# A first MLP block begun pair of heads by pair of heads, with two PSUM banks for the early scores and a new order of instructions

## The chip, the cores and the metric

The kernel runs on one core of a Trainium2 chip. The metric is the device time of one execution in microseconds (us). Its engines are named as the profile names them: PE (TensorE) with its weight loads (PEld), DVE (VectorE), ACT (ScalarE), POOL (GpSimd) and SP (SyncE), whose queue issues most of the DMAs. PE writes its results to PSUM, which has eight banks; the program calls them `bank[0]` to `bank[7]` and the profile calls all of them `pb`.

## What is computed

Four batches of 576 positions go through local attention, a convolutional gated MLP, and a Fourier mix with a second MLP. Cut to what matters:

```python
def attention(q, k, v):                    # (4, 8, 576, 64)
    scores = matmul(q, k.T) / sqrt(64)
    # heads 0-3: the last 32 keys; heads 4-7: 32 keys at distances 0, 4, 8, ...
    scores = where(mask, scores, -1e9)
    a = exp(scores - scores.max(-1))
    return matmul(a / (a.sum(-1) + 1e-9), v)

def first_mlp(x, w_in, conv_w, w_out):     # x (4, 576, 512), w_in (512, 1024)
    h = relu(x @ w_in)
    c = conv3(h, conv_w)                   # along the positions, each of 1024 columns by itself
    return (h * sigmoid(c)) @ w_out

def second(x, w_ch1, w_ch2):               # w_ch1 (512, 2048)
    u = x + real(fft(fft(x, axis=1), axis=2))
    un = (u - mean(u)) / sqrt(var(u) + 1e-6)
    return u + relu(un @ w_ch1) @ w_ch2
```

The weights come as 64-bit floats. Matrix products are made of three products of rounded parts: each operand is split into a high part and a low part (`h`, `l`), and high x high, high x low and low x high are added up.

## The kernel before, in words

**Attention in ticks.** `tick` (L586) handles one piece of a pair of heads: 3 ticks for each of a batch's two plain pairs and 4 for each of its two dilated pairs, 14 a batch, numbered 0 to 55. A tick is a chain: PE adds the mask and the scores into a bank (`sb`); ACT copies them to a tile `sm` (one of a ring of five; from batch 2 on DVE does this and adds the mask); POOL takes the maximum over the partitions into `mx`; DVE subtracts; ACT takes the exponential; PE multiplies with V into a second bank (`pb`); ACT and DVE make the reciprocal `rs`; ACT (L627) or DVE (L624) scales into `xb`; PE transposes; ACT writes the high part of `x` and DVE the low part. A batch's `x` is a tile `xT[b]` of four pairs, `xT[b][:, c]` for pair c. Pair 0 comes from ticks 0 to 2, pair 1 from 3 to 5, pair 2 from 6 to 9, pair 3 from 10 to 13.

**First MLP.** `mlp1` (L1109) goes through eight blocks f of 128 columns. `m1(b, f)` (L666) multiplies `x` with the weight tile (0, f) in two halves of 288 positions. A half is four pairs c times three products, twelve matmuls of 128x288, added up in one bank, which ACT evicts with a relu into `hp`. ACT and DVE then make the convolution `cv`, the gate `g` and the split product `hid`. `m2(b, f)` (L695) multiplies `hid` with the weight tile (1, f) into the accumulators in banks 4 to 7, over all eight f; after the last one they are copied out (`evac`, L742). The sixteen weight tiles are converted from 64 bits, by `Weights.convert` (L534): three DVE steps on `raw` and `win`, a copy to `wf` on ACT or POOL, and a DVE subtraction into the low part of `wf`. Two `raw` tiles take turns.

**Banks.** `of(group, ids)` (L481) hands out banks in turn. The first 16 ticks (`EARLY`, L1092) take their scores in banks 0, 2, 3 and 4 and their second products in 1, 5, 6 and 7; later ticks use bank 0, and 1 and 3. `m1` uses bank 2 in the batches 0 to 2.

**Order.** The program first lists all its work as `Work` entries, with the tiles that each reads and writes, and then a planner (`Plan.order`, L306) lays them out. An entry has engines that could do it, an estimated duration and a key, its due time; `products` (L257) gathers the matmuls made under it into one entry, so that they stand together on PE and wait together. `urgency` (L299) lowers keys so that an entry is due before those that need it. The planner simulates the engines and gives each free one, among the entries that are ready, the one with the lowest key. Then each engine's instructions are issued in that order, and on the chip each waits for what it needs. Between two passes of `urgency` the keys are shaken: each number of `NUDGES` (L188) seeds a random stretch of time and an amplitude, and keys in that stretch are moved by a random amount. The list is what a search over seeds has left.

The times that set the keys here are `at = 1.6 * n` for the ticks of batch 0, `T0 - 8 + 66 / 14 * m` for tick m of batch 1, and

```python
T0 = 42.0
PER = 69.0
        step = PER / NF1
            at = T0 + PER * b + step * f
            m1(b, f, h_banks, at)
            m2(b, f, at + 2 * step)
```

Most of the profile's lines are helpers: L253 is every DVE, ACT and POOL operation recorded by `run`, L266 every PE operation, L295 every DMA. Tiles tell them apart: `pb<-QT,KT` and `pb<-maskt,ident` are scores, `pb<-VT,sm` the second product of a tick, `pb<-ident,xb` its transposes, `pb<-x,wf` is `m1`, `pb<-wf,hid` is `m2` and the last product of the second MLP.

Of the kernel before, what the change touches and what calls it, by code (L numbers as in the profile page):

```python
# [182 lines left out]
class Work:  # L183
# [1 line left out]

NUDGES = (9, 12, 27, 33, 49, 53, 82, 92, 98, 130, 181, 284, 297, 353, 473,  # L188
          503, 521, 594, 836, 1456, 1870, 2106, 2119, 2189, 2250, 2504, 2667, 2792, 3014, 3080,
          3211,)  # L190


LAT = {"PE": 0.25, "DVE": 0.12, "ACT": 0.15, "POOL": 0.2, "SP": 0.0, "NO": 0.0}
# [5 lines left out]
class Plan:  # L199
# [79 lines left out]
    def mm3(self, o, ah, al, bh, bl, first, last):  # L279
        self.mm(o, ah, bh, first, False)  # L280
        self.mm(o, ah, bl, False, False)
        self.mm(o, al, bh, False, last)
# [23 lines left out]
    def order(self):  # L306
        W = self.works
        for w in W:
            w.succ, w.left, w.ready, w.start = [], len(w.deps), 0.0, None
        for w in W:  # L310
            for d in w.deps:
                W[d].succ.append(w.id)
        self.urgency()
        for seed in NUDGES:
            rng = random.Random(seed)
            a = rng.uniform(0, 560)
            z = a + rng.uniform(4, 50)
            amp = rng.choice((1, 2, 4, 8))
            for w in W:
                if a < w.key < z:  # L320
                    w.key += rng.uniform(-amp, amp)
        self.urgency()
        free = dict.fromkeys(("PE", "DVE", "ACT", "POOL", "SP", "NO"), 0.0)
        can = {e: {} for e in free}
        bus, drift = 0.0, 0.0
        out = []

        def can_wait(w, end):
            return w.key < 1e8 and end < w.key + min(w.where.values()) + drift

        def offer(w):
            for e in w.where:
                can[e][w.id] = w
        for w in W:
            if not w.left:
                offer(w)
        while any(can.values()):
            best = None
            for e, c in can.items():
                if c:  # L340
                    t = max(free[e], min(w.ready for w in c.values()))
                    if best is None or t < best[0]:
                        best = t, e
            t, e = best
            pick = None

            wait = WAIT.get(e, 0.0)
            for w in sorted((w for w in can[e].values() if w.ready <= t + wait + 1e-9), key=lambda w: w.key):
                late = False
                for e2, us in w.where.items():  # L350
                    if e2 != e:
                        queue = sum(x.where[e2] for x in can[e2].values()
                                    if x.key < w.key and x.ready <= t and len(x.where) == 1)
                        if max(free[e2], t) + queue + us < t + w.where[e] - 1e-9 and not (
                                us < w.where[e] and can_wait(w, t + w.where[e] + 0.5)):
                            late = True
                if not late:
                    pick = w
                    break
            if pick is None:  # L360

                free[e] = min([f for x, f in free.items() if f > t + 1e-9] + [t + 0.3])
                continue
            w = pick
            for x in w.where:
                del can[x][w.id]
            t = max(t, w.ready)
            w.start, w.eng = t, e
            if e == "PE":
                drift += 0.1 * (t - w.key - drift)  # L370
            end = t + w.where[e]
            free[e] = end
            if w.bytes:
                begin = max(bus, end)
                bus = begin + w.bytes / 265e3
                end = bus + 2.0
            out.append(w)
            for s in w.succ:
                x = W[s]
                lat = 0.0 if w.bytes else LAT[e] if e not in x.where else 0.0  # L380
                x.ready = max(x.ready, end + lat)
                x.left -= 1
                if not x.left:
                    offer(x)
        assert len(out) == len(W), [w.id for w in W if w.start is None][:5]
        return out
# [51 lines left out]
def tile_kernel(ctx: ExitStack, tc: tile.TileContext, forms, qt_in, ktp, ktd, vtp, vtd, wm1, wm2, conv_w,  # L438
# [3 lines left out]
    P = Plan({"ACT": nc.scalar, "DVE": nc.vector, "POOL": nc.gpsimd, "PE": nc.tensor, "SP": nc.sync})  # L442
    mm, mm3, dma = P.mm, P.mm3, P.dma
# [11 lines left out]
    def copy(out_, in_, engines=("ACT",), key=None):  # L455
        n = out_.n()
        psum = in_.tile.pool is banks
        t = {"ACT": on_act(n), "DVE": on_dve(n, False, psum), "POOL": on_pool(n)}
        P.run({e: t[e] for e in engines}, "copy", key, out=out_, in_=in_)

    def dve(op_, us, key=None, **kw):
        P.run({"DVE": us}, op_, key, **kw)

    def lo_of(out_, src, hi, key=None):
        n, psum = out_.n(), src.tile.pool is banks
        dve("tensor_tensor", on_dve(n, True, psum), key, out=out_, in0=src, in1=hi.bitcast(F32), op=ALU.subtract)
# [14 lines left out]
    def of(group, ids):  # L481
        i = turns.get(group, 0)
        turns[group] = i + 1
        return bank[ids[i % len(ids)]]
# [84 lines left out]
    def kq_load(u):  # L569
        b, hp = divmod(u, 4)  # L570
        kt, qt = KT[u % NS], QT[u % NS]
        i = 2 * b + hp % 2
        dma(kt[:, 0:608] if hp < 2 else kt, ktp[i] if hp < 2 else ktd[i])
        dma(qt[0:64, 0, :], qt_in[u, 0:64])
        dma(qt[64:128, 1, :], qt_in[u, 64:128])
# [7 lines left out]
    xT = {b: x_even if b % 2 == 0 else x_odd for b in range(B)}  # L583
# [82 lines left out]
    def m1(b, f, h_banks, at):  # L666
        s = NF1 * b + f
        w = W1.tiles[0, f]
        hp = hpad[s % 2]
        for half in range(2):  # L670
            o = of("h", h_banks)[:, :HS]
            sl = slice(HS * half, HS * half + HS)
            with P.products(at + 4.3 * half):
                for c in range(4):
                    wsl = slice(128 * c, 128 * c + 128)
                    mm3(o, w[:, 0, wsl], w[:, 1, wsl], xT[b][:, c, 0, sl], xT[b][:, c, 1, sl], c == 0, c == 3)
            P.run({"ACT": 0.41}, "activation", out=hp[:, 1 + HS * half:1 + HS * half + HS], in_=o, func=AF.Relu,
                  scale=0.5)
        cv, g = cv_t, g_t
        P.run({"ACT": 0.78}, "mul", out=cv, in_=hp[:, 1:S + 1], mul=convw[:, NF1 + f:NF1 + f + 1])  # L680
        dve("scalar_tensor_tensor", 0.81, out=cv, in0=hp[:, 0:S], scalar=convw[:, f:f + 1], in1=cv,
            op0=ALU.mult, op1=ALU.add)
        dve("scalar_tensor_tensor", 0.88, out=cv, in0=hp[:, 2:S + 2],
            scalar=convw[:, 2 * NF1 + f:2 * NF1 + f + 1], in1=cv, op0=ALU.mult, op1=ALU.add)
        P.run({"ACT": 0.69}, "activation", out=cv, in_=cv, func=AF.Tanh)
        dve("scalar_tensor_tensor", 0.54, out=g[:, 0:289], in0=cv[:, 0:289], scalar=1.0, in1=hp[:, 1:290],
            op0=ALU.add, op1=ALU.mult)
        dve("scalar_tensor_tensor", 0.48, out=g[:, 289:576], in0=cv[:, 575:288:-1], scalar=1.0,
            in1=hp[:, 576:289:-1], op0=ALU.add, op1=ALU.mult)
        gh, gl = hid[s] = gh_t[s % 2], gl_t[s % 2]  # L690
        gs = g.rearrange("p (t s) -> p t s", t=2)
        copy(gh, gs, ("ACT", "POOL"))
        lo_of(gl, gs, gh)
# [394 lines left out]
    for k in range(2 * NF1):  # L1088
        _, i, f = W1.todo[k]
# [5 lines left out]
    def ticks(b):  # L1095
        for m in range(14):
            n = 14 * b + m
            u, t = subs[n]
            if t == 0 and u >= NS:
                kq_load(u)  # L1100
                v_load(u)
            if n < EARLY:
                sb, pb = of("s", [0, 2, 3, 4]), of("v", [1, 5, 6, 7])
            else:
                sb, pb = bank[0], of("v2", [1, 3])
            at = 1.6 * n if b == 0 else T0 + PER * (b - 1) - LEAD + m * (PER - 3.0) / 14
            tick(n, sb, pb, at, b < 2)

    def mlp1(b, f0, f1, h_banks):  # L1109
        step = PER / NF1  # L1110
        for f in range(f0, f1):
            at = T0 + PER * b + step * f
            m1(b, f, h_banks, at)
            m2(b, f, at + 2 * step)

    ticks(0)
    for b in range(3):
        ticks(b + 1)
# [31 lines left out]
    at, begin = T5, {}  # L1150
# [10 lines left out]
    for k, (r, f) in enumerate(seq):  # L1161
# [13 lines left out]
        at, step = begin[r, f]  # L1175
# [85 lines left out]
```

## Time and profile before

| | |
|---|---|
| median of 3 runs | 759.14 us (757.48 to 759.53) |
| the profiled execution's own time | 757.01 us |
| its span, first to last instruction | 755.2 us |
| PE busy | 736.6 us, 98% |
| DVE busy | 478.3 us, 63% |
| ACT busy | 309.8 us, 41% |
| POOL busy | 144.7 us, 19% |
| mean granted clock of TensorE | 0.995 of 2.4 GHz |

The profile is of one execution. Busy shares are means over stages that differ: attention of batch 0 lasts to about 41 us, the first MLP's batch 0 from there to about 120, its other batches with their attention to about 340, and from there on the Fourier mix and the second MLP follow. A row of the timeline gives the start, the duration, the operation with its output and inputs, a count where like instructions stand together, and in brackets how long the engine sat idle before it and what ended that. A stretch gives the engine's busy time with the number of instructions; PEclk is the granted clock as a share of 2.4 GHz.

### The profile page before, as it was taken

Reading aid. Unit: us, or ns where it says so; the run is one execution under the profiler, and the core shown is the slowest. Engines: PE = TensorE matmul, PEld = TensorE weight load, DVE = VectorE, ACT = ScalarE, POOL = GpSimd, SP = SyncE. Lnnn points to the kernel's source line nnn. Section 1 sums busy time; section 2 is a strip of 40 time slices with the busy share of each in tenths; the row PEclk is TensorE's granted clock in tenths of the full one; section 3 lists DMA queues with packets and bytes.
Section 4 is the critical chain, followed back from the end, with each engine's and each line's share of the span. In section 5 each row is a group of like instructions: output and inputs, shape, how many; then the busy total and the mean of one; then the engine's idle time right before and its main releaser. Section 6 shows DMA issues by size and latency. Waiting matters only on the chain.

```text
span 755.2 us, 11432 instructions
## 1 busy us (share of the span) xinstructions
PE 736.6 (98%) x4246; PEld 641.1 (85%) x4246; DVE 478.3 (63%) x1087; ACT 309.8 (41%) x800; POOL 144.7 (19%) x159
## 2 busy tenths in 40 slices
PE   6899999999999999999999999999999999999997
PEld 5798889998999999887888888888888888888896
DVE  5999999989997699998787765362722122111211
ACT  4877877765777564554331322131221101110111
POOL 4865434543653112001000000000000000000000
PEclk9989999999999999999999999999999999999999
DMA  9955454324313543479657331230320012100100
GB/s 257 264 146 165 143 163 145 103 64 163 128 50 101 189 162 114 156 270 306 219 190 259 114 133 62 62 101 6 112 55 2 1 40 72 29 0 1 70 1 28
DMA packets 38077, 87.75 MB, mean 116 GB/s; under 512 B 4351, under 2 KB 8963, under 8 KB 37894
## 3 DMA queue, kind: packets, MB, share of 16 engines
q1 hardware_dynamic: 37222, 83.78, 34.8%
q0 software_dynamic: 432, 2.97, 1.1%
q8 instruction: 33, 0.54, 0.3%
q10 hardware_dynamic: 368, 0.28, 0.1%
q14 instruction: 22, 0.18, 0.1%
HBM read 64.96 MB, written 21.91 MB: 115 GB/s over the span
## 4 chain that ended last, share of the span: by engine, by line
PE 54%; DVE 1%; issue 0%
PE pb L266 54%; DVE fo L253 0%; DVE ns L253 0%; DVE fs L253 0%; DVE hp L253 0%; DVE o L253 0%; DVE f L253 0%; DVE a L253 0%
## 5 line engine op out<-in xcount | busy, mean ns | idle before, releaser
L266 PE MATMUL pb<-wf,hid 128*128 128x512 f32 x1140 | 290.8, 395 | 0.8 <-DVE hid L253 0.8
L266 PEld LDWEIGHTS pb<-wf,hid 128*128 128x128 f32 x1140 | 207.7, 188 | 39.9 <-DVE hid L253 2.0
L253 DVE SCALAR_TENSOR_TENSOR hid<-pb,hid 128x512 fp32r<-128x512 f32 (+1 forms) x80 | 51.0, 637 | 183.3 <-ACT hid L253 183.2
L253 ACT ACTIVATE hid<-pb 128x512 fp32r<-128x512 f32 (+1 forms) x80 | 44.5, 556 | 248.2 <-PE pb L266 231.8
L266 PE MATMUL pb<-x,wf 128*128 128x288 f32 x768 | 115.4, 300 | 0.5 <-ACT hp L253 0.5
L266 PEld LDWEIGHTS pb<-x,wf 128*128 128x128 f32 x768 | 106.9, 189 | 3.0 <-ACT hp L253 0.7
L266 PE MATMUL pb<-unt,wf 128*128 128x512 f32 (+1 forms) x504 | 103.5, 354 | 0.0
L253 POOL PARTITION_ALL_REDUCE mx<-sm x56 | 88.3, 1591 | 62.5 <-ACT sm L253 26.8
L266 PEld LDWEIGHTS pb<-unt,wf 128*128 128x128 f32 x504 | 85.0, 189 | 14.2
L266 PE MATMUL pb<-wf,wf 128*128 128x512 f32 x336 | 82.0, 391 | 0.0
L266 PEld LDWEIGHTS pb<-wf,wf 128*128 128x128 f32 x336 | 62.4, 188 | 12.8
L253 DVE SCALAR_TENSOR_TENSOR cv<-hp,convw,cv 128x576 f32<-128x576 f32 x64 | 56.3, 880 | 1.8 <-ACT cv L253 1.1
L627 ACT ACTIVATE xb<-pb,rs 72x64 f32<-72x64 f32 (+1 forms) x196 | 44.4, 306 | 4.8 <-DVE rs L253 4.7
L266 PE MATMUL pb<-QT,KT 128*104 128x144 f32 (+1 forms) x224 | 44.3, 323 | 1.1 <-DMA QT<-in_qt_dram 0.5
L266 PEld LDWEIGHTS pb<-VT,sm 104*72 104x72 f32 (+1 forms) x448 | 40.1, 156 | 6.2 <-ACT sm L253 4.0
L266 PE MATMUL pb<-VT,sm 104*72 104x65 f32 (+1 forms) x448 | 42.2, 239 | 2.8 <-ACT sm L253 2.8
L266 PEld LDWEIGHTS pb<-QT,KT 128*104 128x104 f32 (+1 forms) x224 | 36.2, 191 | 6.2 <-issue 3.7
L253 ACT ACTIVATE hp<-pb 128x288 f32<-128x288 f32 x64 | 26.2, 412 | 28.2 <-PE pb L266 27.6
L253 DVE TENSOR_TENSOR sm<-sm,mx 104x288 f32<-104x288 f32 (+1 forms) x56 | 32.1, 574 | 8.5 <-POOL mx L253 8.2
L253 DVE TENSOR_TENSOR wf<-raw,wf 128x512 fp32r<-128x512 f32 x44 | 32.5, 738 | 6.0 <-ACT wf L253 5.7
L253 POOL CAST g<-hid 128x64 fp32r<-128x64 f32 x48 | 25.1, 532 | 53.4 <-ACT hid L253 28.9
L253 DVE SCALAR_TENSOR_TENSOR win<-raw,win 128x512 int32<-128x512 int32 x48 | 34.0, 709 | 1.1
(143 smaller groups left out, 849.5 us busy)
## 6 DMA issues: line engine op xcount, KB each, us to landing
raw<-in_wm_dram SPq DMA_DIRECT2D x48, 512.0 KB, 3.9
y<-yd SPq DMA_DIRECT2D x18, 256.0 KB, 2.6
ud<-y SPq DMA_DIRECT2D x18, 256.0 KB, 3.7
QT<-in_qt_dram SPq DMA_DIRECT2D x31, 144.0 KB, 3.8
fd<-fs SPq DMA_DIRECT2D x8, 514.0 KB, 5.3
fl<-fd SPq DMA_DIRECT2D x8, 514.0 KB
yd<-y SPq DMA_DIRECT2D x16, 256.0 KB, 2.0
uu<-ud SPq DMA_DIRECT2D x16, 256.0 KB, 4.4
```

The source lines that it names most:

```text
L253: getattr(self.engines[eng], name)(**a)
L266: getattr(self.engines["PE"], name)(*[v.real() for v in a], **kw)
L627: nc.scalar.mul(out=x[:, i], in_=p[:, i], mul=r[:, i:i + 1])
```

## The change

`m1` makes the half's twelve matmuls in four entries of three, one for each pair of heads, in the first block of all (`s == 0`, which is b = 0 and f = 0); every other block keeps one entry of twelve. All four entries have the same key as the one before. That block uses the banks 2 and 3, one for each half, and the early scores have two banks, 0 and 4, in place of four. `NUDGES` has new seeds, 28 in place of 31, in one round; a round is followed by `urgency`, as the whole list was before. Any number of rounds could stand there.

```diff
-NUDGES = (9, 12, 27, 33, 49, 53, 82, 92, 98, 130, 181, 284, 297, 353, 473,
-          503, 521, 594, 836, 1456, 1870, 2106, 2119, 2189, 2250, 2504, 2667, 2792, 3014, 3080,
-          3211,)
+NUDGES = ((1, 4, 11, 21, 28, 38, 71, 121, 146, 218, 301, 318, 335, 337, 373,
+           393, 395, 442, 453, 491, 962, 1006, 1056, 1064, 1067, 1110, 1610, 1678,),)
...
         self.urgency()
-        for seed in NUDGES:
-            rng = random.Random(seed)
...
-        self.urgency()
+        for seeds in NUDGES:
+            for seed in seeds:
+                rng = random.Random(seed)
...
+            self.urgency()
...
         for half in range(2):
             o = of("h", h_banks)[:, :HS]
             sl = slice(HS * half, HS * half + HS)
-            with P.products(at + 4.3 * half):
-                for c in range(4):
-                    wsl = slice(128 * c, 128 * c + 128)
-                    mm3(o, w[:, 0, wsl], w[:, 1, wsl], xT[b][:, c, 0, sl], xT[b][:, c, 1, sl], c == 0, c == 3)
+
+            for cs in ((0,), (1,), (2,), (3,)) if s == 0 else (range(4),):
+                with P.products(at + 4.3 * half):
+                    for c in cs:
+                        wsl = slice(128 * c, 128 * c + 128)
+                        mm3(o, w[:, 0, wsl], w[:, 1, wsl], xT[b][:, c, 0, sl], xT[b][:, c, 1, sl], c == 0, c == 3)
...
             if n < EARLY:
-                sb, pb = of("s", [0, 2, 3, 4]), of("v", [1, 5, 6, 7])
+                sb, pb = of("s", [0, 4]), of("v", [1, 5, 6, 7])
...
-            m1(b, f, h_banks, at)
+            m1(b, f, [2, 3] if b + f == 0 else h_banks, at)
```

## Rows read from the trace of the kernel before

**Rows 1.** The page's head: the span, and each engine's busy time.

```profile
span 755.2 us, 11432 instructions
PE 736.6 (98%) x4246; PEld 641.1 (85%) x4246; DVE 478.3 (63%) x1087; ACT 309.8 (41%) x800; POOL 144.7 (19%) x159
```

**Rows 2.** The chain of waits in order of time: start, us, what.

```profile
344.20 406.98 PE pb L266 x1967
```

**Rows 3.** Busy time by stretch: stretch, its length, engines (instructions), PEclk, DMA share, GB/s.

```profile
26.00:36.00 10.00, 8.20 (x79) 7.23 (x78) 9.71 (x30) 9.27 (x37) 7.72 (x6) 1.00 1.02 283
36.00:43.00 7.00, 5.84 (x33) 5.62 (x32) 6.30 (x15) 4.69 (x18) 5.68 (x5) 0.51 0.82 231
...
18.00:57.00 39.00, 35.67 (x299) 33.45 (x297) 36.87 (x87) 31.68 (x111) 28.15 (x22) 0.91 0.76 205
57.00:119.30 62.30, 59.47 (x422) 53.29 (x422) 60.20 (x119) 48.03 (x139) 25.71 (x25) 1.00 0.47 148
119.30:345.00 225.70, 223.62 (x1505) 202.72 (x1506) 200.22 (x456) 141.61 (x381) 78.76 (x97) 1.00 0.43 144
```

**Rows 4.** The timeline of DVE: start, us, instruction, idle before and its end.

```profile
19.94 0.68 DVE L253 SCALAR_TENSOR_TENSOR raw<-raw,win 128x512 uint32<-128x512 uint32 x1
...
25.60 0.65 DVE L253 TENSOR_TENSOR wf<-raw,wf 128x512 fp32r<-128x512 f32 x1
...
28.50 0.35 DVE L253 TENSOR_TENSOR x<-pb,x 128x192 fp32r<-128x192 f32 x1
...
33.84 0.41 DVE L253 TENSOR_TENSOR x<-pb,x 128x144 fp32r<-128x144 f32 x1
...
40.66 0.42 DVE L253 TENSOR_TENSOR x<-pb,x 128x144 fp32r<-128x144 f32 x1 [0.56 <-ACT x L253]
...
118.57 0.72 DVE L253 TENSOR_TENSOR wf<-raw,wf 128x512 fp32r<-128x512 f32 x1
```

**Rows 5.** PE's groups from 26 to 41.3: busy, mean ns, idle before and its end.

```profile
L266 PE MATMUL pb<-VT,sm 104*72 104x65 f32 x49 | 4.6, 240 | 0.3 <-ACT sm L253 0.3
...
L266 PE MATMUL pb<-ident,xb 72*128 72x72 f32 x16 | 2.8, 264 | 1.5 <-DVE rs L253 0.9 <-ACT xb L627 0.6
L266 PE MATMUL pb<-VT,sm 128*96 128x65 f32 x8 | 1.5, 372 | 1.2 <-ACT sm L253 1.2
```

**Rows 6.** The timeline of PE.

```profile
26.86 0.29 PE L266 MATMUL pb<-maskt,ident 104*104 104x288 bf16 x1
...
31.07 0.32 PE L266 MATMUL pb<-maskt,ident 128*128 128x384 bf16 x1
...
41.32 2.66 PE L266 MATMUL pb<-x,wf 128*128 128x288 f32 x12
...
44.61 1.85 PE L266 MATMUL pb<-x,wf 128*128 128x288 f32 x12
...
67.01 0.50 PE L266 MATMUL pb<-wf,hid 128*128 128x512 f32 x1 [0.52 <-DVE hid L253]
```

**Rows 7.** The timeline of ACT.

```profile
27.55 0.40 ACT L253 COPY sm<-pb 104x288 f32<-104x288 f32 x1
...
31.15 0.38 ACT L253 COPY sm<-pb 104x288 f32<-104x288 f32 x1
...
46.50 0.41 ACT L253 ACTIVATE hp<-pb 128x288 f32<-128x288 f32 x1
```

**Rows 8.** What DVE waited for, 18 to 119.3: us in total, times, longest.

```profile
DVE x L253 <- ACT x L253: 0.8, 2, 0.6
DVE rs L253 <- ACT rs L253: 0.8, 3, 0.4
DVE hid L253 <- ACT hid L253: 0.7, 1, 0.7
```

**Rows 9.** The timeline of POOL.

```profile
19.98 4.08 POOL L253 PARTITION_ALL_REDUCE mx<-sm  x3 [2.64 <-ACT sm L253]
23.93 0.71 POOL L253 CAST wf<-raw 128x512 fp32r<-128x512 f32 x1
```

More of the change, by code (lines that the diff above doesn't have):

```diff
@@ L313, in order @@
         self.urgency()
-        for seed in NUDGES:
-            rng = random.Random(seed)
[L316 to L321, printed above, removed]
-        self.urgency()
+        for seeds in NUDGES:
+            for seed in seeds:
+                rng = random.Random(seed)
+                a = rng.uniform(0, 560)
+                z = a + rng.uniform(4, 50)
+                amp = rng.choice((1, 2, 4, 8))
+                for w in W:
+                    if a < w.key < z:
+                        w.key += rng.uniform(-amp, amp)
+            self.urgency()
         free = dict.fromkeys(("PE", "DVE", "ACT", "POOL", "SP", "NO"), 0.0)
```

## The prediction

> **What bounds the kernel now.** I read the page's head first: PE is busy 736.6 of 755.2 us [rows 1], so at most 18.6 us can go without taking matmuls away, and the change takes none away. The chain of waits came second: from 344.20 to the end it is one PE piece of 406.98 us [rows 2]. Nothing the change touches lies there, so a gain has to arise before and has to survive up to that point. Third came the table by stretch [rows 3]. From 119.3 to 345 PE is busy 223.62 of 225.70 us, so it alone is the bound there, and whatever is won earlier is handed through. From 18 to 119.3 the picture is another: DVE is busy 36.87 of 39.00 us and then 60.20 of 62.30, PE 35.67 and 59.47. Both are full, and each stands idle only where the other is late. In that stage DVE converts the sixteen tiles of the first MLP's weights; its last conversion ends at 118.57 + 0.72 [rows 4], and the last block's second product cannot start before it.
>
> The reader should see two losses of PE in that stage. From 26 to 36 it is busy 8.20 of 10 us and from 36 to 43 it is busy 5.84 of 7, which makes 2.96 us of gaps; the groups of lines name what ended them (ACT's `sm` 0.3 and 1.2, `rs` 0.9 and `xb` 0.6) [rows 3, 5]. And from 36 to 43 the granted clock is 0.51, the lower level of 1.2 GHz, after the stretch with the gaps, in which it was 1.00 [rows 3]. The first block's matmuls show both levels: twelve take 2.66 us at 41.32 and twelve take 1.85 us at 44.61 [rows 6].
>
> **The change, part by part.**
>
> *The first block in pieces.* In the kernel before, the twelve products of each half are one work that needs all four pairs of heads. The last of them is written at 40.66 + 0.42 = 41.08 [rows 4], and the block begins at 41.32 [rows 6]. After the change a pair's six products (three a half, two halves) need only that pair and the weight tile. The tile is ready at 25.60 + 0.65 = 26.25; the second pair at 28.50 + 0.35 = 28.85; the third at 33.84 + 0.41 = 34.25 [rows 4]. The first pair was there before the tile. So 18 of the 24 products can run between 26.25 and 41: 18 x 1.85/12 = 2.8 us [rows 6], against 2.96 us of gaps. After 41.08 six products are left, 0.9 us, where there were 3.7. No matmul is added; the pieces only split a wait into four.
>
> *The clock.* 5.84 us of PE work ran at about half speed [rows 3], which costs 2.9 us. If the gaps are filled, PE does not go into 36 with gaps behind it, and I expect that loss to go, or most of it. The two together, 2.8 + 2.9 = 5.7 us, are the ceiling of the gain; the floor from this part alone is nothing.
>
> *Two banks for early scores.* A score may start once the score two before it has been copied out, where it was four before. The first score that this holds back is the fourteenth: it began at 26.86 [rows 6], and the twelfth is copied at 27.55 + 0.40 [rows 7]. Its own copy comes at 31.15 [rows 7], because the five `sm` buffers are taken until then; so it has 3 us to spare and costs nothing. The three scores after it, the last of them at 31.07 [rows 6], move to 31 to 36, into the gaps, and leave their place to the first two pairs' pieces. What is late next, if that cover goes, is ACT's copy into `sm` and then POOL's maximum. Bank 3 also serves later ticks, but only after the block has left it: nothing.
>
> *What the early end of the block sets going.* ACT's second relu stands at 46.50 [rows 7]; with six products left it can come some 3.5 us earlier. Behind them stand DVE's two convolution steps and the gate. But DVE is full there, so they only displace weight conversions.
>
> *The new order.* Which instruction stands before which on every queue, SP's and POOL's among them, is new. No row shows what that costs. From below, a better order could take all of DVE's idle time between 18 and 119.3, 2.13 + 2.10 = 4.2 us [rows 3]; from above, a piece may stand in the wrong place (third rival). I put it at nothing beyond the next step, since the loads issued before 41 are the same ones.
>
> *What is kept.* PE's head start of up to 5.7 us at 43 is worth only what DVE can follow. A PE that is ahead in this stage runs into the next missing `hid` or weight tile: the order before shows the pattern with 0.52 us of waiting at 67.01 [rows 6]. DVE's work up to 119.3 stays the same, so it can gain no more than its 4.2 us of idle time. Of that, the waits that ACT's results ended, behind PE's, are 0.8 + 0.8 + 0.7 = 2.3 us [rows 8]; those a faster PE can remove, the rest are gaps of its own. So I keep 2.3 us. The ends are 0.8 (only the wait for `x`, in the slow stretch) and 4.2 (all of it).
>
> A rule that speaks against the pieces stands in the Trainium skill, TensorE: Matmul & The Clock Gate, "Step-by-step: what each phase is for": weights may be pulled ahead, but the matmuls stay in program order. By it a piece that waits for its tile holds every matmul behind it, and by the sum above, which takes each piece to be ready when its turn comes, it holds none. No row of the kernel before shows a matmul held in this way.
>
> **The sum.** The profiled execution took 757.0 us with a span of 755.2, some 2.1 below the median of the runs shown, 759.14. Against its own time: 757.0 - 2.3 = 754.7. Against the median: 759.1 - 2.3 = 756.8 us, own range 754.9 to 758.3.
>
> **The rivals.**
>
> *All of it is kept.* DVE would have to move work behind 119.3, or PE find matmuls that need nothing from DVE, such as scores and second products of the next batch. For it: DVE has some room after 119.3 (200.22 busy of 225.70 [rows 3]). Against it: the accumulators' first round cannot end before the sixteenth tile. It gives 759.1 - 5.7 = 753.4. Chance 0.20.
>
> *The pieces fill nothing.* Their key is that of the whole block, 42, behind the early scores, and the planner prices every matmul at full speed, so its picture of the gaps is not the chip's. It may put the pieces at 38 to 41, where they gain at most a microsecond, and DVE's order stays as full as it is. It gives 758.1 to 759.1, and up to 760 if the order's other moves cost a little. Chance 0.16.
>
> *Slower: a piece waits at PE's head.* Its place is PE's queue between 18 and 36. The tile's upper half is a POOL copy; its input was ready at 19.94 + 0.68 = 20.62 [rows 4], but POOL was in three maxima from 19.98 for 4.08 us and began the copy at 23.93 [rows 9]: 3.3 us in which the tile depends on what POOL takes first. If the planned order counts on the early end and the chip gives the late one, PE stands up to 3.3 us, the ticks behind it and so DVE with it: 759.1 + 3.3 = 762.4. It decides once PE's waits for `wf` or `x` before 41 add up to more than the 3 us of gaps they replace. Against it: the pieces rank behind the ticks' own matmuls. Chance 0.12.
>
> **How the numbers follow.** A measurement of this kernel can tell about 0.3%, 2.3 us, from no change: faster means under 756.9, slower over 761.4. The forecast has 0.52; it lies on that edge, and I count 0.27 of it below and 0.25 above. Faster: 0.27 + 0.20 = 0.47. Same: 0.25 + 0.16 = 0.41. Slower: 0.12. The range goes from 753.6, near the end of the first rival, to 760.0, which takes in the second; the third and a little of the first are left out, under 2 in 10.
>
> **What would show it.** Right: matmuls `x,wf` in groups of three or six between 26 and 41, six left after the last pair; a granted clock above 0.51 from 36 to 43; PE ahead by 4 to 5 us at 50, and DVE's last weight conversion only 1 to 3.5 us earlier than 118.57, with PE's waits for `hid` longer by the difference. The gain at 345 is then that of the last conversion. Wrong: the last conversion moves by as much as PE does (DVE was no bound), the clock still falls to half (the gaps were not its cause), or the pieces stand with waits for `wf` before them.

## The result and the profile after

The changed kernel takes 766.96 us (764.95 to 768.18, three runs) against 759.14: 1.0107 times the time before, with a 95% interval of 1.0089 to 1.0125. It is slower by 7.8 us, where 2.3 us of gain were forecast, and outside the range. The profiled execution took 768.18 us with a span of 766.4, 11.2 longer than the span before. It is the slowest of the three and has the lowest mean clock (0.984, beside 0.989 and 0.991), so its rows show somewhat more than the median.

First the page's head, which answers to [rows 1].

```profile
span 766.4 us, 11473 instructions
PE 743.3 (97%) x4246; PEld 648.2 (85%) x4246; DVE 481.0 (63%) x1090; ACT 305.1 (40%) x795; POOL 144.5 (19%) x161
```

PE is busy 743.3 us where it was 736.6, with the same 4246 matmuls, and idle 23.1 where it was 18.6. So 6.7 of the 11.2 us are matmuls that ran slower and 4.5 are waiting. The table by stretch says where; its stretches are those of [rows 3], and one from 43 to 57 in two halves. That stretch of the kernel before is the last row.

```profile
26.00:36.00 10.00, 8.71 (x86) 8.07 (x85) 9.83 (x27) 7.97 (x30) 7.81 (x8) 1.00 0.93 237
36.00:43.00 7.00, 6.57 (x61) 5.86 (x59) 6.12 (x18) 6.26 (x25) 4.51 (x4) 1.00 0.76 232
...
43.00:50.00 7.00, 6.34 (x39) 5.67 (x37) 6.09 (x15) 5.62 (x21) 7.00 (x5) 0.65 0.73 175
50.00:57.00 7.00, 6.45 (x38) 6.06 (x38) 3.92 (x10) 5.18 (x22) 3.27 (x4) 0.50 0.67 203
...
57.00:119.30 62.30, 56.11 (x369) 50.86 (x369) 56.01 (x104) 37.16 (x110) 24.54 (x26) 0.93 0.43 131
119.30:345.00 225.70, 225.70 (x1533) 206.65 (x1532) 199.83 (x451) 141.79 (x387) 80.27 (x96) 1.00 0.42 135
```

```profile
43.00:57.00 14.00, 14.00 (x117) 13.57 (x116) 13.17 (x24) 10.81 (x35) 8.73 (x8) 1.00 0.41 119
```

Up to 43 the picture is the forecast one: from 36 to 43 the clock is 1.00 and PE busy 6.57, where it was 0.51 and 5.84. The loss comes after. From 43 to 57 the clock is 0.65 and 0.50, where it was 1.00 with PE busy throughout, and DVE, which must not rest in this stage, is busy only 3.92 us of the second 7. An estimate of what the low clock costs, from these rows, is 6.34 x 0.35 + 6.45 x 0.50 + 56.11 x 0.07 = 9.4 us, against 5.84 x 0.49 = 2.9 from 36 to 43 in the kernel before [rows 3]: 6.5 us more, nearly all of the 6.7. From 57 to 119.3 DVE is busy 56.01 us where it was 60.20, PE 56.11 where it was 59.47. From 119.3 on PE has no gap at all: the distance is made by then and handed through.

The timeline of PE shows what was done in that stretch. These are the rows of the first MLP's products, `x,wf` for its first product and `wf,hid` for its second; they answer to [rows 6]. The last row is the first `wf,hid` of the kernel before.

```profile
33.86 1.03 PE L265 MATMUL pb<-x,wf 128*128 128x288 f32 x6
...
40.12 0.64 PE L265 MATMUL pb<-x,wf 128*128 128x288 f32 x3
...
58.38 0.81 PE L265 MATMUL pb<-x,wf 128*128 128x288 f32 x3
...
68.31 1.82 PE L265 MATMUL pb<-x,wf 128*128 128x288 f32 x12
...
74.26 3.42 PE L265 MATMUL pb<-x,wf 128*128 128x288 f32 x24
...
83.24 3.25 PE L265 MATMUL pb<-x,wf 128*128 128x288 f32 x12 [2.86 <-ACT hp L252]
86.28 3.70 PE L265 MATMUL pb<-wf,hid 128*128 128x512 f32 x9
```

```profile
56.40 0.63 PE L266 MATMUL pb<-wf,hid 128*128 128x512 f32 x2
```

Six and three matmuls stand in early gaps, as they should: the first three pairs of the first half. But the last three of that half come at 58.38, and the second half does not come before 74. The first `wf,hid` is at 86.28; in the kernel before it was at 56.40. In between PE works on ticks of batch 1.

Which bank is which does not show in the profile's rows, but it does in the program's order of PE instructions. Here are the lines on bank 3 (`pb_129`; bank 2 is `pb_128`) from place 100 to 148 of that order, where a place is a group of like matmuls:

```
103 L265 MATMUL pb_129<-VT,sm 96x65 x4
110 L265 MATMUL pb_129<-ident,xb 128x96 x2
114 L265 MATMUL pb_129<-VT,sm 72x65 x4
121 L265 MATMUL pb_129<-ident,xb 128x72 x2
125 L265 MATMUL pb_129<-VT,sm 72x65 x4
131 L265 MATMUL pb_129<-ident,xb 128x72 x2
135 L265 MATMUL pb_129<-VT,sm 72x65 x4
139 L265 MATMUL pb_129<-ident,xb 128x72 x2
141 L265 MATMUL pb_129<-VT,sm 72x65 x4
145 L265 MATMUL pb_129<-ident,xb 128x72 x2
148 L265 MATMUL pb_129<-x,wf_144 128x288 x12
```

The second half of the first block (148) stands behind the last tick of batch 1 that uses bank 3 (145). That is no accident of the search. The program lists `ticks(1)` ahead of `mlp1(0, ...)`, and the planner takes the order of listing as the order of use of a tile. Ticks from number 16 on take bank 3 in turn for their second product, the odd ones of batch 1 up to 27. So the block that was to begin early has to wait for a batch of attention that was meant to run beside it. `urgency` then makes it worse: since the block is due at 42, all those ticks become due before 42, ahead of batch 0's own last tick. Batch 0's `x` takes eight writes for its dilated pairs, and the eighth of that kind ends at 57.24 + 0.41 on DVE, where it ended at 41.08; hence the last three products of the first half at 58.38. What this second effect costs by itself, no run separates.

DVE pays. The waits of DVE from 43 to 60 (us in total, times, longest) are those of the ticks' chain, from POOL's maximum to ACT's results:

```profile
DVE sm L252 <- POOL mx L252: 1.8, 2, 1.1
DVE rs L252 <- ACT rs L252: 1.6, 1, 1.6
DVE x L252 <- ACT x L252: 0.6, 2, 0.5
```

Ticks run one behind another, with nothing of the first MLP to put between. The timeline of DVE, which answers to [rows 4], has the late write of `x` and the first and the last of the sixteen weight conversions:

```profile
33.03 0.87 DVE L252 TENSOR_TENSOR wf<-raw,wf 128x512 fp32r<-128x512 f32 x1
...
57.24 0.41 DVE L252 TENSOR_TENSOR x<-pb,x 128x144 fp32r<-128x144 f32 x1
...
128.96 0.69 DVE L252 TENSOR_TENSOR wf<-raw,wf 128x512 fp32r<-128x512 f32 x1 [0.54 <-POOL wf L252]
```

The last of the sixteen conversions ends at 129.65 where it was 119.29. That is 10.4 us, beside 11.2 that the span grew, but the one does not set the other: in e8 below the last conversion ends at 129.42 with a span of 762.0, and in e6 at 124.51 with a span of 756.5.

### The profile page after: what moved, and what is told of

The parts are those of the page before. It is cut to its first block, busy times and chain, and to the rows that moved or that the text cites. A ratio compares the mean times of both kernels' runs of the same rounds, so it can differ in the third digit from the quotient of the medians.

```text
span 766.4 us, 11473 instructions
## 1 busy us (share of the span) xinstructions
PE 743.3 (97%) x4246; PEld 648.2 (85%) x4246; DVE 481.0 (63%) x1090; ACT 305.1 (40%) x795; POOL 144.5 (19%) x161
## 4 chain that ended last, share of the span: by engine, by line
PE 92%; DVE 3%; DMA 1%; ACT 1%; POOL 1%; issue 1%; ACTq 0%; POOLq 0%
PE pb L265 92%; POOL mx L252 1%; DVE sm L252 1%; DMA raw<-in_wm_dram 1%; DMA QT<-in_qt_dram 1%; DVE win L252 1%; ACT sm L252 1%; DVE x L252 0%; DVE cv L252 0%; ACT x L252 0%; DVE wf L252 0%; POOL wf L252 0%; DVE raw L252 0%; DVE fo L252 0%; ACT xb L627 0%
## 5 line engine op out<-in xcount | busy, mean ns | idle before, releaser
L265 PE MATMUL pb<-wf,hid 128*128 128x512 f32 x1140 | 287.3, 394 | 0.0
L265 PEld LDWEIGHTS pb<-wf,hid 128*128 128x128 f32 x1140 | 209.9, 189 | 39.7
L252 POOL PARTITION_ALL_REDUCE mx<-sm x56 | 84.3, 1527 | 52.5 <-DVE sm L252 27.6
L265 PE MATMUL pb<-VT,sm 104*72 104x65 f32 (+1 forms) x448 | 44.7, 248 | 5.9 <-DVE x L252 3.3
L265 PEld LDWEIGHTS pb<-VT,sm 104*72 104x72 f32 (+1 forms) x448 | 42.2, 164 | 9.5 <-ACT sm L252 6.9
L252 DVE SCALAR_TENSOR_TENSOR raw<-raw,win 128x512 uint32<-128x512 uint32 x48 | 34.5, 719 | 0.6
```

What stands on the lines that cost most here:

```text
L252: getattr(self.engines[eng], name)(**a)
L265: getattr(self.engines["PE"], name)(*[v.real() for v in a], **kw)
```

## The experiments

Two theories were set against each other: **bank** (the listing of the block behind the ticks that share bank 3) and **seeds** (the structure is harmless and the new list of seeds a bad one), with the pieces and the two score banks as further suspects. Twelve kernels ran. The table has them in groups; the fourth column is the start of the first `wf,hid`, and the last is where the program's own planner puts PE's end. Each ratio is against runs of the kernel before beside it, with medians of 758.43 us for e1 to e4, 758.29 for e5 to e8 and 758.08 for e9 to e12. The plan itself has the changed kernel 3.7 us behind the kernel before, about half of the 7.8.

| kernel | median us | against before, 95% | first `wf,hid` | planner's end |
|---|---|---|---|---|
| before | 759.14 | | 56.4 | 753.1 |
| changed | 766.96 | 1.0107 (1.0089 to 1.0125) | 86.3 | 756.8 |
| e1 before, no seeds | 767.86 | 1.0124 (1.0100 to 1.0147) | 58.0 | 760.0 |
| e2 changed, no seeds | 773.73 | 1.0192 (1.0170 to 1.0214) | 86.4 | 767.0 |
| e3 listed first, no seeds | 766.15 | 1.0092 (1.0065 to 1.0119) | 55.8 | 761.4 |
| e4 before + bank 3, no seeds | 771.72 | 1.0172 (1.0146 to 1.0198) | 85.3 | 765.6 |
| e5 before + bank 3, own seeds | 769.38 | 1.0151 (1.0134 to 1.0168) | 87.8 | 760.1 |
| e6 listed first, searched | 759.24 | 1.0018 (1.0004 to 1.0032) | 54.0 | 751.7 |
| e7 before, searched again | 760.53 | 1.0030 (1.0017 to 1.0043) | 57.6 | 752.2 |
| e8 changed, searched again | 764.17 | 1.0086 (1.0070 to 1.0101) | 82.6 | 757.0 |
| e9 before + two score banks | 758.84 | 1.0009 (0.9997 to 1.0020) | 59.1 | 754.5 |
| e10 before + pieces | 759.82 | 1.0015 (1.0001 to 1.0029) | 60.0 | 754.7 |
| e11 before, light DVE | 755.87 | 0.9957 (0.9941 to 0.9972) | 57.3 | |
| e12 e6, light DVE | 753.01 | 0.9937 (0.9913 to 0.9960) | 52.8 | |

### The structure without seeds: e1 to e4

The seeds were searched for one structure each, so a kernel that mixes them says little. The first four have none.

```diff
-NUDGES = (9, 12, 27, ...)
+NUDGES = ()
```

> The kernel before with its list of seeds emptied, so that its order is the planner's first draft: the base for the next three, which have no seeds either. Both theories: slower than the kernel before by what its search had won, 5 to 9 us (765 to 768), first m2 at about 55 us as before.

> The changed kernel with its seeds emptied. Theory bank (the change's structure is at fault: the first block's second half writes bank 3, and since that block is listed after the ticks of batch 1, which use bank 3 too, it has to come after all of them): slower than e1 by 5 to 10 us, second half of the first block after 68 us, first m2 after 80. Theory seeds (the structure is harmless, the new seeds are bad): within 2 us of e1 or faster, first m2 at about 55.

e3 lists the first block's `m1` (its products with their relu, convolution and gate) ahead of the ticks of batch 1 and changes nothing else of e2:

```diff
     ticks(0)
+    m1(0, 0, [2, 3], T0)
     for b in range(3):
...
-            m1(b, f, [2, 3] if b + f == 0 else h_banks, at)
+            if b + f:
+                m1(b, f, h_banks, at)
```

> As e2, but the first block is listed ahead of the ticks of batch 1, so that those wait for it in bank 3 and not it for them; pieces, two score banks and bank 3 stay. Theory bank: within 2 us of e1, first m2 at about 55, pieces at 28 to 41. Rival theory pieces or score banks (these cost the time): stays near e2.

e4 is e1 with one thing of the change:

```diff
-            m1(b, f, h_banks, at)
+            m1(b, f, [2, 3] if b + f == 0 else h_banks, at)
```

> The kernel before without seeds, and one thing of the change alone: the second half of the first block goes to bank 3. No pieces, four score banks. Theory bank: slower than e1 by 4 to 9 us, first m2 after 80. Rival theory pieces or score banks: within 1 us of e1.

Measured: 767.86, 773.73, 766.15 and 771.72 us. The structure costs 5.9 us without any seeds (e2 against e1), bank 3 alone 3.9 us (e4 against e1, just short of the 4 expected, and with a range that overlaps e2's), and with the listing turned round pieces, score banks and bank 3 together cost nothing (e3 against e1, 1.7 us the other way, with ranges that overlap). The first `wf,hid` follows the listing in every one of them: past 85 in e2 and e4, at 55.8 and 58.0 in e3 and e1. In e2 the loss is all waiting: PE is busy 740.6 us where it is 740.4 in e1, and idle 31.0 where it is 24.6; no slower matmuls are added there, as they are in the changed kernel. The theory of the seeds falls as the main cause: what they changed is 6.8 us of gain on the changed structure (773.73 to 766.96) and about 9 on the one before (767.86 to 758.43 beside it). The difference, some 2 to 3 us of the 7.8, remains with them.

### Bank 3 alone on the kernel before: e5

The edit is that of e4, on the kernel before with its own seeds.

> The kernel before with its own seeds, and the second half of the first block in bank 3 as the only edit. Theory bank: slower than the kernel before by 5 to 10 us, first m2 after 80 us. Rival theory (bank 3 costs only where there are no seeds): within 2.3 us of it. Part of the loss may be that these seeds were searched for another plan; e6 and e8 bound that part.

769.38 us, 11.1 above the kernel before on the same chip and just over the 5 to 10 expected; the edit has no piece and no new seed in it. The timeline of PE:

```profile
53.41 3.25 PE L266 MATMUL pb<-x,wf 128*128 128x288 f32 x12
...
83.61 3.25 PE L266 MATMUL pb<-x,wf 128*128 128x288 f32 x12 [4.81 <-ACT hp L253]
87.84 3.03 PE L266 MATMUL pb<-wf,hid 128*128 128x512 f32 x12
```

The first half comes at 53.41 in place of 41.32, the first second product at 87.84, and PE stands 4.81 us for `hp` ahead of 83.61, as it stood 2.86 in the changed kernel. This one line of the change is enough for a loss of that size. How much of its 11.1 us comes of seeds searched for another plan is not separated here: without seeds the same line costs 3.9 (e4), while e9 and e10 below put other edits under the same seeds and lose at most 1.7.

### The same search on three structures: e6 to e8

A greedy search went through seeds in order and kept one if the planner's end of PE came earlier, equally long for each. (Such a search on the changed structure, from seed 1 on, gives its list of 28 seeds, number for number, before it finds a 29th.) Only `NUDGES` differs from e3, the kernel before and the changed kernel.

> The changed kernel with the first block listed ahead of the ticks of batch 1, and with seeds searched for that listing; the search keeps a seed if the planner's own end of PE comes earlier. Theory bank: with the listing mended the pieces fill gaps as predicted: 753 to 758, clock above 0.9 from 36 to 43, first m2 at 52 to 56. Rival (pieces give nothing even then): equal to e7.

> The kernel before with nothing changed but the seeds, from an equally long search: the control for e6. Theory bank: 756 to 760, since its first block still waits for all four pairs and the clock still falls after 36. Rival (a longer search is all it needs): as fast as e6.

> The changed kernel with nothing changed but the seeds, from the same search. Theory bank: no order mends it, since the wait for batch 1's ticks is in the listing: 764 to 769, first m2 at about 80 or later. Theory seeds (its list of seeds was an unlucky one): 756 to 760.

759.24, 760.53 and 764.17 us. Another search takes the changed kernel from 1.0107 to 1.0086 times the kernel before, with intervals that overlap, and the first `wf,hid` stays at 82.6: the wait is in its listing. Against e7, the kernel before after the same search and half a us above its expected range, e8 is 3.6 us slower. So the structure costs 5.9 us without seeds and 3.6 with equal searches; the rest of the 7.8 is the lists of seeds. The mended listing reaches the kernel before to within 1 us but does not pass it, missing its expected 753 to 758; against e7, its control, it is 1.3 us ahead with intervals that overlap. So pieces, score banks and bank 3 together are worth between nothing and a little. e6's table by stretch shows where the gain goes:

```profile
26.00:36.00 10.00, 9.72 (x96) 9.29 (x95) 9.76 (x28) 8.50 (x33) 7.50 (x7) 1.00 0.99 271
36.00:43.00 7.00, 6.89 (x58) 6.11 (x57) 6.75 (x16) 6.28 (x22) 5.45 (x4) 1.00 0.63 199
...
43.00:57.00 14.00, 12.50 (x95) 11.21 (x94) 13.91 (x25) 11.03 (x37) 8.26 (x9) 1.00 0.61 187
...
57.00:119.30 62.30, 58.00 (x392) 50.95 (x391) 60.15 (x114) 42.52 (x128) 26.02 (x24) 0.97 0.44 136
...
71.00:78.00 7.00, 4.36 (x36) 3.48 (x35) 6.97 (x14) 5.59 (x19) 4.85 (x5) 0.95 0.53 169
78.00:85.00 7.00, 7.00 (x44) 6.65 (x44) 6.71 (x13) 3.75 (x12) 3.94 (x3) 0.81 0.34 108
```

From 26 to 43 it does all that was predicted of the pieces: PE's gaps are 0.39 us where they were 2.96, and the clock is 1.00 throughout. Then it is given back: from 43 to 57 PE's gaps are 1.50 us where there were none, and from 57 to 119.3, with DVE as busy as before (60.15 us, before 60.20), they have grown from 2.83 to 4.30. From 71 to 78 PE is busy 4.36 of 7 us while DVE is busy 6.97. PE has run ahead (at 71 it has done twelve `x,wf` and two `wf,hid` more than the kernel before), and ACT ends its waits: 1.0 us for `sm`, 1.0 for `hp` and 0.6 for `xb`. From 78 to 85, behind that gap, the clock is 0.81. PE's busy time over the whole span ends at 736.7 us, against 736.6 before.

### The other two parts, alone: e9 and e10

```diff
-                sb, pb = of("s", [0, 2, 3, 4]), of("v", [1, 5, 6, 7])
+                sb, pb = of("s", [0, 4]), of("v", [1, 5, 6, 7])
```

> The kernel before with its own seeds; early scores in banks 0 and 4 alone, nothing else. Theory bank: 0 to 3 us slower than the kernel before (its seeds were searched for four banks), first m2 at about 56. Rival (two score banks are a large part of the loss): slower by over 4 us.

e10 has the loop over `cs` of the change in `m1`, and bank 2 for both halves.

> The kernel before with its own seeds; the first block in pieces, both halves in bank 2 one after the other, four score banks. Theory bank: within 3 us of the kernel before, first half's pieces at 28 to 41, first m2 before 60. Rival (the pieces themselves hold PE's queue): slower by over 4 us, PE waiting for wf or x before 41.

758.84 and 759.82 us beside 758.08: no difference that can be told for the score banks, and 1.7 us for the pieces under seeds that are not theirs, with an interval that begins at 1.0001. The first second product starts at 59.1 and 60.0, some 3 us later than in the kernel before and a little past what was expected, but far from 85.

### A lighter DVE: e11 and e12

```diff
+            n = len(P.works)
             dve("tensor_scalar", 0.45, out=win, ...)
             dve("scalar_tensor_tensor", 0.74, out=win, ...)
+            if self.src is wm1 and self.at > 1:
+                for x in P.works[n:]:
+                    x.fn = lambda _: None
```

The order stays that of the kernel before and of e6; the two steps are planned and not issued. They are the ones that put the upper word of each 64-bit weight into `win`, so the fifteen tiles take all but the lowest three bits of each weight from the first tile. (The expectation has it the other way round.)

> The kernel before in the same order, with the two steps that fill win left out on DVE for fifteen of the first MLP's sixteen weight tiles (the low bits of these weights come out of another tile's): some 16 us less of DVE work before 119. If DVE bounds the stage: 3 to 8 us faster than the kernel before. If PE alone bounds it: within 1 us.

> As e6, with the same two steps left out. If DVE is what takes the pieces' gain back: 3 to 6 us faster than e11, since PE's filled gaps and its full clock then come through. If the gain goes elsewhere: level with e11, as e6 was about level with the kernel before.

755.87 and 753.01 us. In e11 DVE's busy time from 57 to 119.3 falls from 60.20 to 50.77, and yet the kernel gains only 2.2 us, short of the 3 expected; PE is then busy 60.72 of 62.30 and has little left to gain there. e12 is 2.9 us ahead of e11, a little under the 3 to 6 expected and with single runs that overlap, where e6 was 1 us behind the kernel before. The same edit is thus worth some 2 us on the kernel before and some 6 on e6 (1.0018 to 0.9937). The two page heads, e11 first:

```profile
PE 736.3 (98%) x4246; PEld 642.1 (85%) x4246; DVE 462.1 (61%) x1057; ACT 309.0 (41%) x800; POOL 142.9 (19%) x159
```

```profile
PE 732.9 (98%) x4246; PEld 638.3 (85%) x4246; DVE 464.3 (62%) x1056; ACT 307.1 (41%) x805; POOL 144.6 (19%) x155
```

PE's busy time differs by 3.4 us, about the 2.9 that the clock's dip was priced at. PE's idle time hardly differs: 17.8 us in e11, 18.3 in e12. So with a lighter DVE the gain comes through as a clock that stays up: its mean is 0.997 to 1.000 in e12's five executions, 0.993 to 0.995 in e11's ten, and 0.993 to 0.999 in e6's twelve. The filled gaps are given back even then. From 71 to 78 e12 shows nearly the gap of e6, with waits ended by ACT as there:

```profile
71.00:78.00 7.00, 4.91 (x44) 4.56 (x45) 7.00 (x14) 5.17 (x18) 6.03 (x5) 1.00 0.51 168
```

Behind it the clock stays at 1.00 from 78 to 85. Why it fell to 0.81 in e6 and not here is not shown. These two kernels compute with other weights, so they are no candidates; no run that keeps the whole computation was faster than the kernel before.

## Why the prediction was wrong

- **The step that failed** is a sentence in the part on the two banks: "Bank 3 also serves later ticks, but only after the block has left it: nothing." It gave no reason for that order; going by due times, the block (42) does come ahead of the first tick of batch 1 on bank 3 (34 + 14 = 48). In this program the order of use of a tile is the order in which the code lists the work, due times only choose among what is ready, and `mlp1(0, ...)` is listed behind `ticks(1)`. The prediction took no account of the order of the calls. e5 prices that line at 11.1 us with the old seeds, e4 at 3.9 without seeds, e2 against e1 the whole structure at 5.9, and e3 takes it away by listing the block first.
- **The new order** was put at nothing, too. With equal searches the structure costs 3.6 us of the 7.8 and without seeds 5.9, so the lists of seeds have a share of some 2 to 4 us.
- **The pieces in the gaps** were right in kind. In the changed kernel nine of the 24 products stood in gaps before 41 and the stretch from 26 to 43 lost 1.72 us to gaps in place of 2.96; in e6, where the listing lets all of them, 0.39.
- **The clock** was right for the stretch it was argued for: 1.00 from 36 to 43, in the changed kernel as in e6. It was no net gain in the changed kernel, whose PE is busy 6.7 us longer, at 0.65 and 0.50 from 43 to 57.
- **Two score banks cost nothing:** right (e9: 1.0009, interval 0.9997 to 1.0020).
- **What is kept:** 2.3 us of 5.7 was too much. In e6, the kernel that the prediction had in mind, nothing is kept against the kernel before, and 1.3 us against e7. The mechanism named, DVE full to about 119, is borne out in part: with a lighter DVE the clock's half of the gain comes through (e12), the gaps' half does not. The sum had DVE's waits shrink and did not reckon that PE, once ahead, makes new gaps (3.0 us more from 43 to 119.3 in e6, against 2.6 won before) and, in e6, a new dip of the clock. Nor is the gain that of the last weight conversion, as the prediction had it: in e6 that conversion is 5.2 us later than in the kernel before and the span 1.3 longer. e11 shows the other side: DVE's work could fall by 9.4 us in that stretch and the kernel gained 2.2, so neither engine alone is the bound.
- **The rivals:** the slower one had the right sign and the wrong place. It looked for a piece waiting in PE's queue for its weight tile, with up to 3.3 us. No row of the changed kernel has PE waiting for `wf` before 41; the tile was late (33.90 in place of 26.25), and the plan had reckoned with it. The rule on matmuls in program order, from the Trainium skill, TensorE: Matmul & The Clock Gate, "Step-by-step: what each phase is for", was not put to the test: no piece stood at PE's head unready for long, the longest such wait, in e3, being 0.24 us.

## What to carry to other kernels

Before a buffer is given to an earlier piece of work, look for every other user of it in the order in which the program lists them: a planner that takes dependences from listing follows that order, whatever the due times say, and passes the due time on to all that stands ahead. Test such a change without the tuned order first, both sides alike, and only then search both again, since a search can be worth as much as the change itself (7 to 9 us here) and may win more on one side than on the other. And where two engines are full in the same stage, look for a filled gap further on: in e6 what was won before 43 was lost again by 119.

## What the runs showed that was not expected

In the changed kernel PE is busy 6.45 of 7 us from 50 to 57, on ticks, and the granted clock is 0.50 (the lower level, 1.2 GHz) all through, while from 26 to 36, with PE busy 8.71 of 10 us, all but 1.0 of it ticks, it is 1.00. What ends such a low stretch was not tried. The planner's end and the measured median are 4.3 (e9) to 10.2 us (changed kernel) apart in the kernels above that issue all of their plan, so a difference of less than some 6 us in the plan need not hold on the chip: e6 was planned 1.4 us earlier than the kernel before and ran 1 us later.
